# Moving the return of the last five token tiles into the first expert's work, the exponential to ScalarE, and the gather into the routing

## The chip, the cores and the metric

The kernel runs on one core of a Trainium2 chip. The metric is the time of one execution in device microseconds (us). A core has five engines, each with an instruction queue of its own that runs strictly in order: TensorE (PE in the profile; PEld is its weight load), VectorE (DVE), ScalarE (ACT), GpSimd (POOL), and SyncE (SP), which here only issues transfers. Transfers run on 16 DMA engines that all queues share.

## The reference

Three stages follow one another on inputs of B=4 sequences, H=8 heads, S=576 positions, D=64:

```python
# 1. attention: a local band of +-3 positions, plus attention over groups of 4 averaged positions
out_d     = softmax(scale * q_d @ k_d.T) @ v_d          # q_d, k_d, v_d: means of 4 positions
out_local = softmax(where(|i-j| < 4, scale * q @ k.T, -1e9)) @ v
x = (repeat(out_d, 4) + out_local) -> rows of N = 2304 tokens by 512
# 2. mixture of 8 experts, two for each token, with noisy gates
logits = x @ w_gate + log1p(exp(x @ w_noise)) * noise
x = sum over the two largest of softmax(two) * (relu(x @ w1[e]) @ w2[e])      # w1 512x1024, w2 1024x512
# 3. mixture of 8 other experts, one for each token
logits = x @ w_gate2 + modality_bias[modality_id]
out = gate * (relu(x @ w1'[e]) @ w2'[e])
```

## The kernel before

**Attention.** The loop at L1114 takes 18 steps; step i prepares head pair i+1, scores pair i and finishes pairs i-1 and i-2. Four pairs make a sequence, two pairs a group g for the loads. The order within a step is written by hand: `transposes(i+1)`, `softmax2(i-1)`, `values(i-2)`, `scores(i)`, `combine(i-2)`, `p_transposes(i-1)`, `softmax1(i)`, `softmax_d1/d2(i)`, and `pool_v`, GpSimd's sum of v over four positions. The result of a sequence collects in `xT` (features by tokens) and is whole after `combine` of its fourth pair.

**Giving x back.** The 18 tiles of 128 tokens go from `xT` to rows. `xback_att(t)` multiplies a tile by `gw` (an identity beside the two gate matrices) with 8 fp32 matmuls, or 16 where a tile spans two sequences, into `px`, which comes from the same pool of two buffers, `psD`, as the scores' `pd`. Its `rest()` runs at the next `flush()`: ScalarE copies the rows to `xr` (two buffers), VectorE sums the logits into `lg`, and a transfer writes `xr` to `x_rows` in DRAM. Before, the dictionaries `before` and `behind` say at which step a tile comes ahead of the scores or at the step's end; tiles 13 to 17 need the last sequence and come after the loop, at L1184.

**Routing.** `route1(c0, c1, ...)` is a generator that emits the routing of half of the tokens in small pieces. `tick(n)` takes n pieces; `Between` wraps VectorE, so that most attention instructions on it are followed by one piece. A piece that yields "PE" holds the generator until `unblock` lets TensorE's part in. Its parts: `softplus` on VectorE, with an exponential by a polynomial; the two largest; `places` on TensorE; `locate`; then 18 pairs of one-hot tiles (`hots`; for the first half `ol` is made on GpSimd, L545) which TensorE inverts into a table. `places_early` decodes the row numbers `idx0` of the first four experts' first 256 tokens, chosen from tiles 0 to 8 alone.

**Experts.** `ffn.run` goes through items, each one expert with some rows, 8 blocks f of F. Its first item has 256 rows, gathered by `ffn.gather` (GpSimd's indirect transfers) from `x_rows`. A block loads and splits weights into `whi`, `wlo`, does `layer1` of the next block and `layer2` of this one; `hook(i, f, half)` is called after `layer1` (half 0), in the middle of `layer2` (half 2) and after it (half 1). In the first four items `hook0` ticks the routing of the second half of the tokens, which must be done before the fifth item gathers its rows.

Of the kernel before, what the change touches and what calls it, by code (L numbers as in the profile page):

```python
# [18 lines left out]
MAGIC = 12582912.0  # L19
M128 = 1610612736.0  # L20

EXP = [1.0, 1.0000000360960746, 0.4999999535047545, 0.1666642092713234, 0.04166772440021678, 0.00837476549703475,
       0.0013859289912904367]
ATANH = [2.0, 0.666664104680626, 0.40021790854867745, 0.2799817325801463, 0.2802763957015976]


# [20 lines left out]
class Attention:  # L47
# [128 lines left out]
        if g % 2 == 0:  # L176
            self.xT[g // 2] = self.xpool.tile([128, 4, self.S], F32, tag="xT", name="xT")

    def pool_v(self, g, part):

        vr, vd = self.gt[g]["vr"], self.gt[g]["vd"]
        for c in range(2):
            self.nc.gpsimd.tensor_tensor(vd[:, c], vd[:, c] if part else vr[c][:, :, 0], vr[c][:, :, part + 1], op=ALU.add)

    def transposes(self, i):
# [157 lines left out]
def softplus(nc, V, pool, z, out, T, E):  # L343

    A = ALU

    def t(n, dt=F32):
        return pool.tile([128, 9, E], dt, tag=f"sp_{n}", name=f"sp_{n}")[:, :T]
    na, n, m, r, p, u, ni = t("na"), t("n"), t("m"), t("r"), t("p"), t("u"), t("ni", I32)

    V.scalar_tensor_tensor(na, z, -1.0, z, op0=A.mult, op1=A.min)
    yield
    V.tensor_scalar(na, na, -86.0, None, op0=A.max)
    yield
    V.tensor_scalar(n, na, 1.4426950408889634, MAGIC, op0=A.mult, op1=A.add)
    yield
    V.tensor_scalar(n, n, MAGIC, None, op0=A.subtract)
    yield
    V.scalar_tensor_tensor(r, n, -0.693359375, na, op0=A.mult, op1=A.add)
    V.tensor_scalar(m, n, 127.0, 8388608.0, op0=A.add, op1=A.mult)  # L360
    yield
    V.scalar_tensor_tensor(r, n, 2.12194440e-4, r, op0=A.mult, op1=A.add)
    V.tensor_copy(ni, m)
    yield
    V.tensor_scalar(p, r, EXP[6], None, op0=A.mult)
    yield
    for k in range(5, 0, -1):
        V.scalar_tensor_tensor(p, p, EXP[k], r, op0=A.add, op1=A.mult)
        yield
    V.scalar_tensor_tensor(p, p, 1.0, ni.bitcast(F32), op0=A.add, op1=A.mult)  # L370
    yield

    V.tensor_scalar(u, p, 2.0, None, op0=A.add)
    yield
    nc.vector.reciprocal(u, u)
    yield
    V.tensor_tensor(r, p, u, op=A.mult)
    yield
    V.tensor_tensor(u, r, r, op=A.mult)
    yield  # L380
    V.tensor_scalar(p, u, ATANH[-1], None, op0=A.mult)
    yield
    for c in ATANH[-2:0:-1]:
        V.scalar_tensor_tensor(p, p, c, u, op0=A.add, op1=A.mult)
        yield
    V.scalar_tensor_tensor(p, p, 2.0, r, op0=A.add, op1=A.mult)
    yield
    V.scalar_tensor_tensor(out, z, 0.0, p, op0=A.max, op1=A.add)
    yield
# [482 lines left out]
def core(ctx, tc, q, k, v, moe_w_gate, moe_w_noise, moe_noise, moe_w1, moe_w2,  # L872
# [42 lines left out]
    with ExitStack() as actx:  # L915
# [65 lines left out]
        def xback_att(t):  # L981
            px = att.psD.tile([128, 2, 512], F32, tag="D", name="px")
            pv = px[:, :, :2 * XB].rearrange("p a (b c) -> p a b c", b=2)
            xr = xback(t, [pv[:, 0], pv[:, 1]])

            def rest():
                nc.scalar.activation(xr, pv[:, :, :, :128], AF.Copy)
                nc.vector.tensor_reduce(lg[:, t], pv[:, :, :, 128:].rearrange("p a b c -> p c a b"), axis=AX.XY, op=ALU.add)
                nc.sync.dma_start(x_rows[128 * t:128 * t + 128, :DM], xr.rearrange("p a b c -> p (a b c)"))
            after.append(rest)  # L990

        def route1(c0, c1, bank, eng, heng, then=None):
# [101 lines left out]
        def places_early():  # L1094

            v, f = (t.rearrange("p (e t) -> p e t", e=E)[:, :NX, :NE0] for t in (tab, fs))
            yield from rt.decode(f, v, rt.padh.rearrange("p (e t) -> p e t", e=E)[:, :NX, :NE0])
            nc.vector.tensor_copy(idx0[:, 0], f)

            d = route.tile([128, NX, NE0], F32, tag="hold2", name="hold2")  # L1100
            nc.vector.tensor_scalar(d, f, float(N), -float(N), op0=ALU.is_ge, op1=ALU.mult)
            yield
            nc.vector.tensor_tensor(idx0[:, 1], d, f, op=ALU.add)
            yield

        att.tick = tick
        NP = 4 * B

        before = {6: 0, 7: 2, 10: 5, 11: 7, 14: 10, 15: 12}
        behind = {6: 1, 7: 3, 9: 4, 10: 6, 11: 8, 13: 9, 14: 11}  # L1110
        small = load_small()
        finish_now(att.transposes(0))
        att.group(0)
        for i in range(NP + 2):  # L1114
            g, ph = divmod(i, 2)
            if ph == 1:
                if g + 2 < 2 * B:
                    att.load_qk(g + 2)
                if g + 1 < 2 * B:
                    att.load_vr(g + 1)  # L1120
            if ph == 0 and i and g < 2 * B:
                att.load_vw(g)
            if 3 <= i <= 7:
# [12 lines left out]
                att.values(i - 2)  # L1136
                att.scale_d(i - 2)
            flush()
            if i == 12:
                back.append(route1(0, HT, att_bank, nc.vector, nc.gpsimd, hold))  # L1140
                back.append(places_early())
            unblock(1)
            if i in before:
                xback_att(before[i])
            if 0 < i < NP:
                att.scores(i)
            if i >= 2:
                att.combine(i - 2)
            flush()
            tick(2)  # L1150
            if 1 <= i <= NP:
                pt = att.p_transposes(i - 1)
                next(pt)
            if 0 < i < NP:
                att.softmax1(i)
            if 1 <= i <= NP:
                finish_now(pt)
            unblock(1)
            if i < NP:
# [1 line left out]
                if ph == 0 and g + 1 < 2 * B:  # L1161
                    att.group(g + 1)
                att.softmax_d2(i)
                for j in ((0, 1), (2,))[ph] if i > 1 else ((), (0, 1, 2))[ph]:
                    att.pool_v(g, j)
            tick(2 if i < NP else 30)
            if i == 9:
                second_bias()
            if i in behind:
                xback_att(behind[i])  # L1170
            if i == 12:

                nc.sync.dma_start(x_rows[N:].rearrange("(a p) c -> p a c", p=128),
                                  zero[:, None, :].to_broadcast([128, 5, XW]))
            if i == 14:
# [1 line left out]
                           [(e, EARLY) for e in range(NX)] + [(e, 640 - EARLY) for e in range(NX)]  # L1177
                           + [(e, 640) for e in range(NX, E)]]
                          + [dict(ns=n, w1=moe2_w1, w2=moe2_w2) for n in [512, 256, 256, 384] + [256] * (STATIC - 1)])

                nc.sync.dma_start(x2_rows.rearrange("(a p) c -> p a c", p=128),
                                  zero[:, None, :YW].to_broadcast([128, NT + 5, YW]))
        ffn.start()
        for t in range(13, NT):  # L1184
            xback_att(t)
            tick(3)
            flush()
            unblock(1)
            tick(6)
        tick(1000, True)  # L1190
        rows0 = ffn.gather(x_rows[:HT * 128, :], [idx0[:, 1, 0, j:j + 1] for j in range(NE0)], "xg0", NE0, axr)
    fpool = ctx.enter_context(tc.tile_pool(name="fpool", bufs=1))
    fps = ctx.enter_context(tc.tile_pool(name="fps", bufs=1, space=PSUM))
    ffn.open(fpool, fps)
# [74 lines left out]
    def ffn_bank():  # L1269
        return fps.tile([128, 512], F32, tag="y3", name="rbank")  # L1270

    def hook0(i, f, half):
        if i == 0 and half == 0 and f == 0:
            back.append(route1(HT, NT, ffn_bank, nc.vector, None))
            back.append(places_known())
        unblock(1)
        tick(1)

# [392 lines left out]
```

## Time and profile before

| | |
|---|---|
| median of three executions | 925.9 us (923.14 to 927.91) |
| the profiled execution | 926.93 us, span 925.2 us |
| busy | PE 94%, PEld 83%, DVE 59%, ACT 46%, POOL 35% |
| mean granted TensorE clock | 0.973 |
| first matmul of the first expert | at 179.99 us of the span |

The page's busy shares are means over stages. The attention and the first routing fill the span up to about 169 us; then come the last five tiles and the first gather, and from 180 us on the experts, with TensorE busy nearly throughout. What the change touches lies between 57 and 270 us.

### The profile page before, as it was taken

To read this page: it belongs to the slowest core of one execution; us is meant where nothing else is said; L and a number is where in the kernel's file an instruction comes from. 1 tells how busy PE (TensorE), PEld (TensorE's weight loads), DVE (VectorE), ACT (ScalarE), POOL (GpSimd) and SP (SyncE) were. 2 spreads that over 40 slices of the span, in tenths; PEclk is the share of its full clock that TensorE was granted. 3 is DMA by queue.
4 is the path that set the end of the run, shared out by engine and by line. 5 is a ranking of instruction groups with operands and counts; after the bars stand their busy time and mean duration, and the time that the engine had idled before them with its cause. 6 is when DMAs were issued, how large, how long until landed. Compare 5 with 4: busy or idle time off the path is not lost. (4 is left out here: it accounts for less than half of the span.)

```text
span 925.2 us, 18236 instructions
## 1 busy us (share of the span) xinstructions
PE 870.4 (94%) x6775; PEld 764.1 (83%) x6775; DVE 550.4 (59%) x1345; ACT 429.0 (46%) x947; POOL 322.3 (35%) x460
## 2 busy tenths in 40 slices
PE   5898977799999999999999999989989999999995
PEld 4777866698888988999898999978867889999994
DVE  6775697489975544554343443434666877556662
ACT  3675644455554534444233342334423356455552
POOL 7876658436553213043106032050020442222210
PEclk9998988899999999999999999999989999999998
DMA  8878659747776457476328245175433467546650
GB/s 175 171 159 189 169 143 329 240 167 229 204 235 195 140 146 181 143 204 147 129 71 182 92 92 162 46 161 161 128 99 109 155 239 245 190 154 220 216 209 24
DMA packets 158702, 153.83 MB, mean 166 GB/s; under 512 B 74319, under 2 KB 119887, under 8 KB 158608
## 3 DMA queue, kind: packets, MB, share of 16 engines
q1 hardware_dynamic: 146528, 120.15, 42.2%
q0 software_dynamic: 12080, 32.45, 15.2%
q8 instruction: 56, 0.92, 0.4%
q14 instruction: 38, 0.31, 0.1%
HBM read 124.98 MB, written 27.85 MB: 165 GB/s over the span
## 5 line engine op out<-in xcount | busy, mean ns | idle before, releaser
L746 PE MATMUL ph<-xh,whi 128*128 128x256 f32 (+3 forms) x768 | 238.4, 310 | 2.8 <-DVE wlo L707 2.1
L746 PE MATMUL ph<-xl,whi 128*128 128x256 f32 (+3 forms) x768 | 237.6, 309 | 0.4 <-DVE xl L732 0.3
L746 PE MATMUL ph<-xh,wlo 128*128 128x256 f32 (+3 forms) x768 | 237.6, 309 | 0.1
L758 PE MATMUL y<-whi,hh 128*128 128x512 f32 x472 | 192.2, 407 | 0.1
L758 PE MATMUL y<-wlo,hh 128*128 128x512 f32 x472 | 188.1, 398 | 0.0
L758 PE MATMUL y<-whi,hl 128*128 128x512 f32 x472 | 187.6, 398 | 0.0
L707 DVE TENSOR_TENSOR wlo<-raw,whi 128x512 fp32r<-128x512 f32 x135 | 93.2, 690 | 157.4 <-ACT whi L706 144.9
L706 ACT ACTIVATE whi<-raw 128x512 fp32r<-128x512 f32 x160 | 101.0, 631 | 170.7 <-PE y L758 155.7
L746 PEld LDWEIGHTS ph<-xh,whi 128*128 128x128 f32 x768 | 146.0, 190 | 12.2 <-issue 2.6
L746 PEld LDWEIGHTS ph<-xl,whi 128*128 128x128 f32 x768 | 145.9, 190 | 8.3 <-DVE xl L732 1.0
L748 ACT ACTIVATE hh<-ph 128x256 fp32r<-128x256 f32 (+3 forms) x192 | 83.2, 433 | 142.3 <-PE ph L746 133.0
L746 PEld LDWEIGHTS ph<-xh,wlo 128*128 128x128 f32 x768 | 146.2, 190 | 1.8 <-DVE wlo L707 0.3
L749 DVE SCALAR_TENSOR_TENSOR hl<-ph,hh 128x256 fp32r<-128x256 f32 (+3 forms) x192 | 92.5, 482 | 84.5 <-ACT hh L748 81.0
L1215 POOL DMA_INDIRECT x_rows<-y,idx x35 | 57.4, 1641 | 208.1 <-ACT y L1206 108.2
L709 DVE TENSOR_TENSOR wlo<-raw,whi 128x512 fp32r<-128x512 f32 x160 | 120.6, 754 | 11.9 <-ACT whi L708 10.9
L758 PEld LDWEIGHTS y<-whi,hl 128*128 128x128 f32 x472 | 89.5, 190 | 21.6 <-DVE hl L749 0.4
L758 PEld LDWEIGHTS y<-whi,hh 128*128 128x128 f32 x472 | 90.2, 191 | 13.6 <-DVE y L1208 0.8
L758 PEld LDWEIGHTS y<-wlo,hh 128*128 128x128 f32 x472 | 89.8, 190 | 12.6
L708 ACT ACTIVATE whi<-raw 128x512 fp32r<-128x512 f32 x160 | 98.6, 616 | 0.0
L732 DVE TENSOR_TENSOR xl<-pt,xh 128x512 fp32r<-128x512 f32 x59 | 38.7, 687 | 30.8 <-ACT xh L731 30.6
L271 POOL TENSOR_TENSOR Pd<-pe,sm 32x380 f32<-32x380 f32 (+1 forms) x48 | 42.1, 877 | 42.8 <-ACT kT L198 10.4
L1215 POOL DMA_INDIRECT out_dram<-y,pi x19 | 20.6, 1084 | 100.6 <-ACT y L1206 44.1
(311 smaller groups left out, 1085.5 us busy)
## 6 DMA issues: line engine op xcount, KB each, us to landing
raw<-in_moe_w_dram SPq DMA_DIRECT2D x160, 512.0 KB
x_rows<-zero SPq DMA_DIRECT2D x1, 5934.0 KB
vr<-in_v_dram SPq DMA_DIRECT2D x16, 288.0 KB
x_rows<-xr SPq DMA_DIRECT2D x18, 256.0 KB
x2l<-x_rows SPq DMA_DIRECT2D x18, 256.0 KB
qk<-in_q_dram SPq DMA_DIRECT2D x32, 128.0 KB
qk<-in_k_dram SPq DMA_DIRECT2D x32, 128.0 KB
vw<-in_v_dram SPq DMA_DIRECT2D x24, 128.0 KB
```

What stands on the lines that cost most here:

```text
L271: eng.tensor_tensor(Pd[s, :, W * g:W * g + n], pe[s, :, :n], sm[s, :, None].to_broadcast([W, 2 * NB, n]), op=ALU.mult)
L706: nc.scalar.activation(h1, a, AF.Copy)
L707: eng.tensor_tensor(l1, a, h1.bitcast(F32), op=ALU.subtract)
L708: nc.scalar.activation(hi[:, 1], r2[:, half], AF.Copy)
L709: nc.vector.tensor_tensor(lo[:, 1], r2[:, half], hi[:, 1].bitcast(F32), op=ALU.subtract)
L732: nc.vector.tensor_tensor(xl, p, xh.bitcast(F32), op=ALU.subtract)
L746: nc.tensor.matmul(ps, w[a][:, k], x[b][:, k, s], start=(i == 0), stop=(i == 3 * KD - 1))
L748: nc.scalar.activation(hh[:, s], ps, AF.Relu)
L749: nc.vector.scalar_tensor_tensor(hl[:, s], ps, 0.0, hh[:, s].bitcast(F32), op0=ALU.max, op1=ALU.subtract)
L758: nc.tensor.matmul(p, h[a][:, 128 * j:128 * j + 128], w[b], start=(f == 0 and i == 0), stop=(f == self.FB - 1 and i == 2))
L1215: d = nc.gpsimd.indirect_dma_start(out=dst, out_offset=bass.IndirectOffsetOnAxis(ap=ix, axis=0), in_=y, in_offset=None, **kw)
```

## The change

- `softplus`: the polynomial and its splitting are replaced by one ScalarE exponential, with three empty pieces after it.
- `rest()` issues the write of `xr` from ScalarE's queue and no longer from SyncE's.
- `between` takes the place of `before` and `behind`: a step's first tile comes between `scores(i)` and `p_transposes(i-1)`, a second one behind `softmax1(i)` and a flush.
- Tiles 13 to 17 leave the end of the attention: `hook0` gives them back in blocks 0 and 1 of the first item, in the banks y2 and y3; the second routing is queued after tile 17.
- `places_early` issues the gather of the first item itself; the first routing is queued at the end of step 12 and not in its middle.
- The zeros of `x2_rows` are written at step 12 and not at step 14; `load_vr` comes ahead of `load_qk`; `pool_v` does one half of the positions in each of the two steps of a group.

```diff
@@ class Attention
-    def pool_v(self, g, part):
+    def pool_v(self, g, c):
         vr, vd = self.gt[g]["vr"], self.gt[g]["vd"]
-        for c in range(2):
+        for part in range(3):
             self.nc.gpsimd.tensor_tensor(vd[:, c], vd[:, c] if part else vr[c][:, :, 0], vr[c][:, :, part + 1], op=ALU.add)
@@ def softplus
     V.scalar_tensor_tensor(na, z, -1.0, z, op0=A.mult, op1=A.min)
     yield
-    V.tensor_scalar(na, na, -86.0, None, op0=A.max)
-    yield
-    V.tensor_scalar(n, na, 1.4426950408889634, MAGIC, op0=A.mult, op1=A.add)
...
-    for k in range(5, 0, -1):
-        V.scalar_tensor_tensor(p, p, EXP[k], r, op0=A.add, op1=A.mult)
-        yield
-    V.scalar_tensor_tensor(p, p, 1.0, ni.bitcast(F32), op0=A.add, op1=A.mult)
-    yield
+    nc.scalar.activation(p, na, AF.Exp)
+    for _ in range(3):
+        yield
@@ def xback_att, rest()
-                nc.sync.dma_start(x_rows[128 * t:128 * t + 128, :DM], xr.rearrange("p a b c -> p (a b c)"))
+                nc.scalar.dma_start(x_rows[128 * t:128 * t + 128, :DM], xr.rearrange("p a b c -> p (a b c)"))
@@ def places_early
             nc.vector.tensor_tensor(idx0[:, 1], d, f, op=ALU.add)
+            rows0.extend(ffn.gather(x_rows[:HT * 128, :], [idx0[:, 1, 0, j:j + 1] for j in range(NE0)], "xg0", NE0, axr))
             yield
@@ the loop of the attention
-        before = {6: 0, 7: 2, 10: 5, 11: 7, 14: 10, 15: 12}
-        behind = {6: 1, 7: 3, 9: 4, 10: 6, 11: 8, 13: 9, 14: 11}
+        between = {6: [0], 7: [1], 8: [2], 9: [3], 10: [4, 5], 11: [6, 7], 12: [8], 14: [9], 15: [10], 16: [11], 17: [12]}
...
             if ph == 1:
+                if g + 1 < 2 * B:
+                    att.load_vr(g + 1)
                 if g + 2 < 2 * B:
                     att.load_qk(g + 2)
-                if g + 1 < 2 * B:
-                    att.load_vr(g + 1)
...
-            if i == 12:
-                back.append(route1(0, HT, att_bank, nc.vector, nc.gpsimd, hold))
-                back.append(places_early())
             unblock(1)
-            if i in before:
-                xback_att(before[i])
             if 0 < i < NP:
                 att.scores(i)
             if i >= 2:
                 att.combine(i - 2)
             flush()
             tick(2)
+            for t in between.get(i, [])[:1]:
+                xback_att(t)
             if 1 <= i <= NP:
                 pt = att.p_transposes(i - 1)
                 next(pt)
             if 0 < i < NP:
                 att.softmax1(i)
+            flush()
+            for t in between.get(i, [])[1:]:
+                xback_att(t)
             if 1 <= i <= NP:
                 finish_now(pt)
...
-                for j in ((0, 1), (2,))[ph] if i > 1 else ((), (0, 1, 2))[ph]:
-                    att.pool_v(g, j)
+                for c in ((0,), (1,))[ph] if i > 1 else ((), (0, 1))[ph]:
+                    att.pool_v(g, c)
             tick(2 if i < NP else 30)
...
-            if i in behind:
-                xback_att(behind[i])
             if i == 12:
+                flush()
+                back.append(route1(0, HT, att_bank, nc.vector, nc.gpsimd, hold))
+                back.append(places_early())
+                nc.sync.dma_start(x2_rows.rearrange("(a p) c -> p a c", p=128),
+                                  zero[:, None, :YW].to_broadcast([128, NT + 5, YW]))
                 nc.sync.dma_start(x_rows[N:].rearrange("(a p) c -> p a c", p=128),
                                   zero[:, None, :].to_broadcast([128, 5, XW]))
             if i == 14:
...
-                nc.sync.dma_start(x2_rows.rearrange("(a p) c -> p a c", p=128),
-                                  zero[:, None, :YW].to_broadcast([128, NT + 5, YW]))
+        flush()
         ffn.start()
-        for t in range(13, NT):
-            xback_att(t)
-            tick(3)
-            flush()
-            unblock(1)
-            tick(6)
         tick(1000, True)
-        rows0 = ffn.gather(x_rows[:HT * 128, :], [idx0[:, 1, 0, j:j + 1] for j in range(NE0)], "xg0", NE0, axr)
@@ hook0
+    T0 = 13
+    def xback_ffn(t):
+        px = [fps.tile([128, 512], F32, tag=f"y{2 + a}", name="px") for a in range(2)]
+        pv = [p[:, :2 * XB].rearrange("p (b c) -> p b c", b=2) for p in px]
+        xr = xback(t, pv)
+        for a in range(2):
+            nc.scalar.activation(xr[:, a], pv[a][:, :, :128], AF.Copy)
+        l2t = route.tile([128, 2, 2 * E], F32, tag="l2t", name="l2t")
+        for a in range(2):
+            nc.vector.tensor_reduce(l2t[:, a], pv[a][:, :, 128:].rearrange("p b c -> p c b"), axis=AX.X, op=ALU.add)
+        nc.vector.tensor_tensor(lg[:, t], l2t[:, 0], l2t[:, 1], op=ALU.add)
+        nc.scalar.dma_start(x_rows[128 * t:128 * t + 128, :DM], xr.rearrange("p a b c -> p (a b c)"))
+        if t == NT - 1:
             back.append(route1(HT, NT, ffn_bank, nc.vector, None))
             back.append(places_known())
     def hook0(i, f, half):
-        if i == 0 and half == 0 and f == 0:
+        t = T0 + 3 * f + (0, 2, 1)[half]
+        if i == 0 and t < NT:
+            xback_ffn(t)
         unblock(1)
         tick(1)
```

## Rows read from the trace of the kernel before

**Rows 1.** Windows: length; PE, PEld, DVE, ACT, POOL busy; granted clock; DMA share; GB/s.
```profile
75.20:87.50 12.30, 8.94 (x150) 7.22 (x148) 7.02 (x21) 6.27 (x22) 7.59 (x10) 0.81 0.89 217
113.80:147.90 34.10, 26.45 (x469) 22.26 (x468) 31.18 (x100) 17.61 (x58) 19.73 (x26) 0.90 0.62 176
147.90:168.70 20.80, 16.64 (x222) 13.42 (x220) 15.31 (x53) 8.98 (x26) 18.07 (x25) 0.84 0.99 340
180.00:206.90 26.90, 26.75 (x162) 24.42 (x163) 19.02 (x44) 13.66 (x27) 8.42 (x8) 0.90 0.60 208
```

**Rows 2.** Timeline of PE: start, duration, line, count, idle before and its releaser.
```profile
53.39 1.31 PE L285 MATMUL pp<-gw,Pd 128*128 128x128 f32 x10 [1.54 <-POOL Pd L271]
...
91.72 1.74 PE L971 MATMUL px<-gw,xT 128*64 128x144 f32 x16
...
105.69 1.25 PE L971 MATMUL px<-gw,xT 128*128 128x144 f32 x8
...
140.53 0.34 PE L213 MATMUL pd<-mask,identB 128*128 128x190 bf16 x2 [1.13 <-DVE lg L988]
...
177.83 1.48 PE L729 MATMUL pt<-gw,xg 128*128 128x128 f32 x8 [3.09 <-DVE lg L988]
179.99 0.58 PE L746 MATMUL ph<-xh,whi 128*128 128x256 f32 x1 [0.69 <-ACT xh L731]
```

**Rows 3.** Timeline of ACT, in the same form.
```profile
55.33 0.53 ACT L235 ACTIVATE pe<-pe 128x380 f32<-128x380 f32 x1
...
66.73 0.65 ACT L987 ACTIVATE xr<-px 128x512 f32<-128x512 f32 x1
...
79.80 0.60 ACT L987 ACTIVATE xr<-px 128x512 f32<-128x512 f32 x1 [4.25 <-DMA x_rows<-xr]
...
146.72 0.26 ACT L1014 ACTIVATE qex<-qex 128x72 f32<-128x72 f32 x1
...
172.59 0.60 ACT L987 ACTIVATE xr<-px 128x512 f32<-128x512 f32 x1 [1.96 <-PE px L971]
...
176.92 0.60 ACT L987 ACTIVATE xr<-px 128x512 f32<-128x512 f32 x1 [1.88 <-DMA x_rows<-xr]
```

**Rows 4.** Timeline of SP's queue: when it issued transfers.
```profile
74.02 0.83 SPq L989 DMA_DIRECT2D x_rows<-xr  x2
...
142.63 0.48 SPq L1181 DMA_DIRECT2D x_rows<-zero  x1
```

**Rows 5.** Timeline of DVE.
```profile
117.00 0.69 DVE L353 TENSOR_SCALAR sp_na<-sp_na 128x72 f32<-128x72 f32 x1
...
124.21 0.22 DVE L370 SCALAR_TENSOR_TENSOR sp_p<-sp_p,sp_ni 128x72 f32<-128x72 f32 x1
...
143.53 0.22 DVE L1011 TENSOR_TENSOR qex<-qnl,tpm 128x72 f32<-128x72 f32 x1
...
146.95 0.27 DVE L515 TENSOR_REDUCE more<-A 128x8 f32<-128x72 bf16 x1
...
168.48 0.17 DVE L1103 TENSOR_TENSOR idx<-hold,fs 128x8 int32<-128x8 f32 x1
```

**Rows 6.** Timeline of POOL.
```profile
146.00 1.78 POOL L545 TENSOR_SCALAR ol<-r_h,lclo 128x128 f16<-128x128 f16 x3 [2.39 <-DVE lclo L536]
147.86 2.81 POOL L271 TENSOR_TENSOR Pd<-pe,sm 32x380 f32<-32x380 f32 x3
...
161.94 4.91 POOL L545 TENSOR_SCALAR ol<-r_h,lclo 128x128 f16<-128x128 f16 x8
169.57 1.39 POOL L720 DMA_INDIRECT xg<-x_rows,idx  x1 [2.72 <-DVE wlo L707]
...
176.54 0.20 POOL L805 COPY meta<-xg 128x16 f32<-128x16 f32 x1 [2.29 <-DMA xg<-x_rows,idx]
```

**Rows 7.** Groups of instructions by line, up to 420 us: busy, mean ns.
```profile
L183 POOL TENSOR_TENSOR vd<-vd,vr 72x256 f32<-72x256 f32 x32 | 22.5, 724 | 0.0
```

**Rows 8.** DMA issues: KB each.
```profile
x_rows<-zero SPq DMA_DIRECT2D x1, 5934.0 KB
```

More of the change, by code (lines that the diff above doesn't have):

```diff
@@ L20 @@
 M128 = 1610612736.0
-EXP = [1.0, 1.0000000360960746, 0.4999999535047545, 0.1666642092713234, 0.04166772440021678, 0.00837476549703475,
-       0.0013859289912904367]
 ATANH = [2.0, 0.666664104680626, 0.40021790854867745, 0.2799817325801463, 0.2802763957015976]
@@ L348, in t @@
         return pool.tile([128, 9, E], dt, tag=f"sp_{n}", name=f"sp_{n}")[:, :T]
-    na, n, m, r, p, u, ni = t("na"), t("n"), t("m"), t("r"), t("p"), t("u"), t("ni", I32)
+    na, r, p, u = t("na"), t("r"), t("p"), t("u")
     V.scalar_tensor_tensor(na, z, -1.0, z, op0=A.mult, op1=A.min)
     yield
-    V.tensor_scalar(na, na, -86.0, None, op0=A.max)
-    yield
-    V.tensor_scalar(n, na, 1.4426950408889634, MAGIC, op0=A.mult, op1=A.add)
-    yield
-    V.tensor_scalar(n, n, MAGIC, None, op0=A.subtract)
-    yield
[L359 to L366, printed above, removed]
-    for k in range(5, 0, -1):
-        V.scalar_tensor_tensor(p, p, EXP[k], r, op0=A.add, op1=A.mult)
+    nc.scalar.activation(p, na, AF.Exp)
+    for _ in range(3):
         yield
-    V.scalar_tensor_tensor(p, p, 1.0, ni.bitcast(F32), op0=A.add, op1=A.mult)
-    yield
     V.tensor_scalar(u, p, 2.0, None, op0=A.add)
@@ L1103, in places_early @@
             nc.vector.tensor_tensor(idx0[:, 1], d, f, op=ALU.add)
+            rows0.extend(ffn.gather(x_rows[:HT * 128, :], [idx0[:, 1, 0, j:j + 1] for j in range(NE0)], "xg0", NE0, axr))
             yield
+        rows0 = []
         att.tick = tick
         NP = 4 * B
-        before = {6: 0, 7: 2, 10: 5, 11: 7, 14: 10, 15: 12}
-        behind = {6: 1, 7: 3, 9: 4, 10: 6, 11: 8, 13: 9, 14: 11}
+        between = {6: [0], 7: [1], 8: [2], 9: [3], 10: [4, 5], 11: [6, 7], 12: [8], 14: [9], 15: [10], 16: [11], 17: [12]}
         small = load_small()
@@ L1270, in ffn_bank, with hook0 @@
         return fps.tile([128, 512], F32, tag="y3", name="rbank")
-    def hook0(i, f, half):
-        if i == 0 and half == 0 and f == 0:
+    T0 = 13
[11 more added lines that the diff above has]
+        if t == NT - 1:
             back.append(route1(HT, NT, ffn_bank, nc.vector, None))
             back.append(places_known())
+    def hook0(i, f, half):
+        t = T0 + 3 * f + (0, 2, 1)[half]
+        if i == 0 and t < NT:
+            xback_ffn(t)
         unblock(1)
```

## The prediction

> **What bounds the kernel now.** I read the page first, then windows by stage, then the timelines of the stretch the change touches, engine by engine, and the SP queue. TensorE is the bound from about 180 us on: in the first expert it is busy 26.75 of 26.9 us [rows 1], so anything added there costs its own time. Before that no single engine is. The attention's steps are a ring of in-order queues: TensorE transposes, VectorE reduces and normalises, GpSimd scales the band (L271), TensorE transposes that, and so on; TensorE waits for GpSimd once a step, 1.54 us in the step shown [rows 2]. From 113.8 to 147.9 us VectorE is the bound, 31.18 of 34.1 us, because the first routing runs on it beside the attention; from there to 168.7 us it is GpSimd, 18.07 of 20.8 us [rows 1]. The row numbers for the first expert are ready at 168.48 + 0.17 = 168.65 us [rows 5], the second of its two gathered tiles is there at 176.54 us [rows 6], and its first matmul starts at 179.99 us [rows 2]. So the path to 179.99 is attention ring, VectorE, GpSimd, gather; the last five tiles lie beside the gather, and only their last 1.3 us (176.54 to 177.83, a wait for `lg`) are on it.
>
> **The change, part by part.** I follow that path and sum the shifts of the first expert's start, then add what the moved tiles cost behind it.
>
> *Steps 6 to 11: -1.8 us (bounds -7 and +4).* Four things.
> (a) ScalarE stood 4.25 us, until 79.80 us, for a buffer of `xr` [rows 3]. The copy that filled the buffer's predecessor had ended at 66.73 + 0.65 = 67.38 us, but SP, busy with the loads of q, k and v, issued its write only at 74.02 us [rows 4]. Issued by ScalarE it leaves 6.6 us earlier, and the wait goes: -4.25. In that stretch the granted clock was 0.81 of full speed, between the 1.2 and 2.4 GHz levels [rows 1]; without the stop I give 0.9 us back as an estimate (12.3 us at 0.19 less speed is 2.3 us of TensorE's time, of which TensorE is not all the step): -0.9.
> (b) Five tiles of these steps stood at a step's end, ahead of the next transposes, at up to 1.25 us [rows 2]. Between scores and band transposes a tile lies in the wait of up to 1.54 us for GpSimd [rows 2]. I take 0.6 us a tile, under half of either: -3.0 (0 to -6.2).
> (c) Now ScalarE copies `xr` and issues the write ahead of its later work in a step, where in even steps the next reductions wait for it. A copy is 0.6 [rows 3], an issue 0.83/2 = 0.4 on SP [rows 4]; no row shows an issue on ScalarE, so 0.3 to 0.9 on the path, twice in single-tile even steps; I take 0.9: +1.8.
> (d) In steps 10 and 11 the second tile finds only one free buffer of `psD`, that of the first tile, since `pd` of this step is still to be read by `softmax_d1`. It waits until ScalarE has passed the exponential, which ends 55.33 + 0.53 - 53.39 = 2.5 us after the band transposes start [rows 2, 3], then 0.6 of `xr` and some 0.3 of `lg`, 3.4 us in all; 1.15 of them TensorE fills with those transposes. +2.2 a step: +4.4 (0 if buffers come otherwise).
> Sum: -4.25 - 0.9 - 3.0 + 1.8 + 4.4 = -1.95; I take -1.8.
>
> *Steps 12 to 14: -7.1 us (bounds -10 and -3).* From the polynomial go 14 VectorE instructions, the first at 117.00, the last at 124.21 us [rows 5], 5.07 us in sum; they overlap by about 0.07 each, so 4.1 us of a saturated engine. In their place ScalarE does one exponential of the same shape as L1014's, 0.26 us [rows 3], hidden in ScalarE's idle half (17.61 of 34.1 us busy) and, for VectorE, behind the three empty pieces; if ScalarE came late, VectorE would stand up to 0.5 us. The routing now starts at the end of step 12, so that its 11 instructions of placing (143.53 to 146.95 us, 2.65 us in sum, 1.9 without overlap) [rows 5] come behind the normalisation of pair 14 and no longer ahead of it. The wait of the scores for `lg`, 1.13 us [rows 2], goes with the tile ahead of them. -4.1 - 1.9 - 1.1 = -7.1.
>
> *GpSimd's tail: +2.1 us (bounds 0 and +4).* From the band scaling at 147.86 us on, GpSimd is full [rows 1]. Three one-hot tiles that ran before it, 1.78 us [rows 6], now come behind it, and so does one more `pool_v` addition, 0.72 us [rows 7], since each step now does three of one half; of the sum, 2.5, I let 0.4 fall into its remaining idle time. Queued behind these on GpSimd are the other one-hot tiles (the last eight take 4.91 us [rows 6]) and then the gather itself, so this is on the path.
>
> *Row numbers to first matmul: -2.3 us (bounds -3.3 and -0.5).* Before: 179.99 - 168.65 = 11.34. The issue by the routing gains nothing by itself: before, GpSimd started the gather 0.92 us after the numbers were ready, with nothing of its own in between. Gone are the 1.3 us until `lg` frees the banks, and the five writes that shared the DMA engines with the second gather. I take 7.0 for the gather (7.89 before) and 2.0 for transposes and splits (2.16 before): 9.0.
>
> So the first expert starts 1.8 + 7.1 - 2.1 + 2.3 = 9.1 us earlier.
>
> *Tiles 13 to 17 in the first expert: +7.1 us (bounds +6 and +17).* TensorE is full there. Tile 13 spans two sequences, 16 matmuls, 1.74 us; four tiles of 8 matmuls are 1.25 each [rows 2]: 6.7. Each needs the banks of the one before; half a `layer2` lies between, so I add 0.4 of stalls. VectorE (19.02 of 26.9 us busy) and ScalarE (13.66) have room [rows 1]. The clock is low for the first part of the expert either way (mean 0.90 [rows 1]), since TensorE stands for the gather in both: 0, perhaps 1.5 either way.
>
> *At nothing:* the second softplus, because TensorE covers VectorE there (26.75 of 26.9 us; were VectorE the bound, up to 4.1 us would be won); the second routing queued four hooks later but with nine pieces less; loads of v ahead of q and k, since SP runs steps ahead; weights of blocks 4 and 5 issued earlier, as TensorE did not wait for weights.
>
> *Sum:* -9.1 + 7.1 = -2.0. The profiled execution, 926.9, becomes 924.9; the median of the runs shown lies 1.0 below that execution, so I predict **924.0 us**.
>
> On (a) the Trainium skill has a rule that speaks against the change: "DMA: Bandwidth & Descriptors", section "Issuing engines are not separate DMA queues", says that all issuers share the same DMA engines and that a second issuer saves only the sequencer's time, usually small. Here the row agrees on the flight but not on "small": of 12.4 us from the copy's end to 79.80, 6.6 were the line at SP. By the rule taken at its word the wait would stay; that is rival four.
>
> **The rivals.**
> 1. *The ring closes up.* (d) does not happen or is filled, and the routing, no longer against a full VectorE, saves more: -5 and -9, within their bounds, in the first two terms instead of -1.8 and -7.1, total -7. For it: TensorE was busy 26.45 of 34.1 us there, so there is room. Against: GpSimd's tail is full already. Time 919.
> 2. *ScalarE held by its own writes in the first expert (slower).* A tile's copy needs the `xr` buffer of two tiles before. A write took 176.92 - 173.19 = 3.7 us from its copy's end to its release [rows 3]. If tiles follow at some 2 us (an estimate: 1.25 and half a `layer2`), the third to fifth each wait; behind the copy stand ScalarE's `whi` and `hh`, and TensorE soon after them. Three full waits are 11.1 us in place of 0.4: total +8.7, 934.6. It decides from a flight above some 5 us, since expert work between the tiles hides about that.
> 3. *The zeros come down on v.* 5.9 MB [rows 8] at 340 GB/s [rows 1] hold the DMA engines for 17.5 us. Before they were issued at 142.63 us [rows 4], beside nothing urgent; now ahead of the last group's loads of v. If these land late, `pool_v` holds GpSimd in step 14, perhaps 5 us: total +3, 929.
> 4. *Writes no sooner.* The 4.25 + 0.9 us of (a) stay: total +3.1, 929.
>
> **How the numbers follow.** 0.5% is 4.6 us, about what a measurement of this kernel can tell from no change. My forecast, own range 919.5 to 928, has 0.40; 0.11 of that lies under 921.3: faster 0.11, same 0.29. Rival 1 has 0.29, nearly all faster: 0.28 and 0.01. Rival 2 has 0.14, slower 0.13, same 0.01. Rival 3 has 0.08, same 0.05, slower 0.03. Rival 4 has 0.09, same 0.06, slower 0.03. Faster 0.39, same 0.42, slower 0.19. The range takes in rival 1 with the bounds of its terms, down to 914.5, and rivals 3 and 4, and stops short of rival 2's full price: to 931.
>
> **What would show it.** The writes of `xr` on ScalarE's queue within 1 us of the copy, and no 4 us wait; scores spaced evenly from step 12 to 15; the row numbers near 162 us; the first L746 matmul near 171 us; in the first expert three tiles in block 0, two in block 1, and the expert's end about 2 us earlier than before. The prediction is wrong if TensorE stands for ScalarE between the tiles, if GpSimd waits for `vr`, or if the routing's end does not move with the attention.

## The result

The changed kernel takes **933.25 us** (median of 6, 929.28 to 936.64), the kernel before beside it 926.89 us: ratio 1.0071, 95% interval 1.0049 to 1.0094. It is slower, by some 6.6 us; the forecast was 924.0 with a range up to 931.0. The execution profiled after took 936.64 us (span 934.9), its own slowest; that of before 926.93 (span 925.2). So stages below add up to +9.7 us, and comparisons of time go by ratios.

The windows of the changed kernel, cut at the scores of steps 6, 12 and 15, at the row numbers, and at the first expert (columns as in [rows 1]):

```profile
60.75:119.88 59.13, 50.96 (x949) 43.41 (x948) 36.66 (x102) 35.54 (x118) 37.78 (x48) 0.97 0.77 191
119.88:151.67 31.79, 24.25 (x455) 20.49 (x454) 24.63 (x73) 15.92 (x54) 18.38 (x23) 0.91 0.87 292
151.67:176.31 24.64, 18.19 (x224) 16.17 (x223) 15.60 (x64) 9.41 (x28) 18.41 (x27) 0.77 0.34 111
185.44:218.60 33.16, 32.84 (x210) 29.83 (x211) 21.09 (x50) 17.24 (x38) 9.43 (x10) 0.92 0.44 151
```

I read every run by the same five landmarks: the starts of the scores' second group of matmuls (`pd<-kT,qT`) in steps 6, 12 and 15, the end of the last `idx<-hold,fs` (row numbers), the first `layer1` matmul, the first `y<-y` on ScalarE (first expert's end). Lengths between them, each in one profiled execution, in us (the stretch from the scores of step 15 to the row numbers is called the tail below):

| kernel | 6 to 12 | 12 to 15 | 15 to row numbers | to first matmul | first expert | ratio to before (95%) |
|---|---|---|---|---|---|---|
| before | 54.63 | 37.21 | 17.35 | 11.34 | 27.07 | 1 |
| changed | 59.13 | 31.79 | 24.64 | 9.13 | 33.19 | 1.0071 (1.0049-1.0094) |
| e1 old places | 51.05 | 32.40 | 25.46 | 8.87 | 33.13 | 1.0026 (1.0012-1.0040) |
| e2 late copy | 63.25 | 31.10 | 25.69 | 9.11 | 32.46 | 1.0139 (1.0117-1.0161) |
| e3 exponential alone | 50.97 | 32.33 | 17.22 | 11.80 | 26.27 | 0.9922 (0.9904-0.9941) |
| e4 five tiles alone | 51.03 | 38.47 | 17.22 | 8.55 | 32.67 | 1.0040 (1.0025-1.0054) |
| e5 old places, zeros | 50.77 | 33.24 | 23.15 | 8.88 | 33.03 | 0.9994 (0.9973-1.0016) |
| e6 old places, queueing | 50.97 | 29.96 | 26.41 | 9.11 | 33.43 | 1.0002 (0.9987-1.0018) |
| e7 old places, zeros, queueing | 50.72 | 32.09 | 18.50 | 8.72 | 33.65 | 0.9926 (0.9895-0.9957) |
| e8 five tiles back | 61.96 | 32.01 | 22.07 | 14.12 | 27.20 | 1.0085 (1.0056-1.0113) |
| e9 second tiles behind | 55.93 | 32.78 | 25.35 | 9.42 | 33.15 | 1.0025 (1.0005-1.0045) |
| e10 exponential, writes | 54.16 | 33.31 | 17.23 | 14.63 | 26.78 | 0.9977 (0.9958-0.9996) |
| e11 exponential, hots split | 54.29 | 31.92 | 16.22 | 12.12 | 27.58 | 0.9881 (0.9859-0.9902) |
| e12 as e7, five tiles back | 51.27 | 31.77 | 18.63 | 14.82 | 26.38 | 0.9920 (0.9898-0.9941) |
| e13 zeros only | 57.53 | 32.41 | 21.88 | 8.82 | 32.46 | 1.0087 (1.0066-1.0109) |
| e14 exponential, late queueing | 53.78 | 32.82 | 21.97 | 11.47 | 26.25 | 0.9941 (0.9920-0.9963) |

Names in the lines below: `Pd` is the band's softmax as GpSimd scales it, `pdT` ScalarE's copy of the transposed dilated softmax, `mxd` the maxima of the dilated scores, `vr` v as loaded and `vd` its sum over four positions, `vw` v as loaded for the band, and `ol` the one-hot tiles, made from `lclo`, a part of each token's place.

Three readings of the changed kernel. First TensorE's timeline; the rows with tiles and waits answer to [rows 2].

```profile
67.11 0.66 PE L193 MATMUL pk<-gw,qk 128*128 128x128 f32 x4 [0.94 <-ACT pdT L294]
...
76.47 0.76 PE L309 MATMUL pva<-pdT,vd 72*64 72x144 f32 x6 [0.88 <-ACT pdT L294]
...
102.96 1.25 PE L952 MATMUL px<-gw,xT 128*128 128x144 f32 x8 [1.90 <-DVE lg L969]
...
113.81 1.25 PE L952 MATMUL px<-gw,xT 128*128 128x144 f32 x8 [1.90 <-DVE lg L969]
...
180.45 1.09 PE L710 MATMUL pt<-gw,xg 128*128 128x128 f32 x4 [5.91 <-DMA xg<-x_rows,idx]
183.65 1.11 PE L710 MATMUL pt<-gw,xg 128*128 128x128 f32 x4 [2.11 <-DMA xg<-x_rows,idx]
185.44 0.58 PE L727 MATMUL ph<-xh,whi 128*128 128x256 f32 x1 [0.69 <-ACT xh L712]
...
190.99 1.74 PE L952 MATMUL px<-gw,xT 128*64 128x144 f32 x16
```

Then ScalarE's in step 6 (answers to [rows 3]):

```profile
65.62 0.61 ACT L968 ACTIVATE xr<-px 128x512 f32<-128x512 f32 x1
66.25 0.35 ACTq L970 DMA_DIRECT2D x_rows<-xr  x1
66.65 0.70 ACT L294 ACTIVATE pdT<-ppd 72x288 f32<-72x288 f32 x2 [0.42 <-ACT xr L968]
```

The tile's copy and the issue of its write stand 1.03 us ahead of `pdT`, for which TensorE waits: 0.94, 0.88, 0.92, 0.87 us in steps 6 to 9, once each. The 4 us wait for an `xr` buffer is gone, as forecast.

Last GpSimd's (answers to [rows 6]):

```profile
149.35 3.21 POOL L269 TENSOR_TENSOR Pd<-pe,sm 32x380 f32<-32x380 f32 x3 [2.87 <-DVE sm L40]
...
154.19 1.79 POOL L526 TENSOR_SCALAR ol<-r_h,lclo 128x128 f16<-128x128 f16 x3 [0.43 <-DVE lclo L517]
...
158.26 3.66 POOL L526 TENSOR_SCALAR ol<-r_h,lclo 128x128 f16<-128x128 f16 x6
162.00 2.54 POOL L269 TENSOR_TENSOR Pd<-pe,sm 32x380 f32<-32x380 f32 x3
...
167.70 4.69 POOL L526 TENSOR_SCALAR ol<-r_h,lclo 128x128 f16<-128x128 f16 x8 [1.35 <-PE rbank L532]
176.61 1.40 POOL L701 DMA_INDIRECT xg<-x_rows,idx  x1 [4.22 <-DVE idx L1084]
```

All ten one-hot tiles of the first batch now come behind the `Pd` of 149.35; before, three of the ten ran ahead of the `Pd` of 147.86 [rows 6]. Nine of them stand ahead of the last `Pd`. The gather leaves at 176.61, in [rows 6] at 169.57.

### The profile page after: what moved, and what is told of

It reads as the page before. It is cut to its first block, busy times and chain, and to the rows that moved or that the text cites. A ratio compares the mean times of both kernels' runs of the same rounds, so it can differ in the third digit from the quotient of the medians.

```text
span 934.9 us, 18191 instructions
## 1 busy us (share of the span) xinstructions
PE 871.1 (93%) x6775; PEld 764.1 (82%) x6775; DVE 544.4 (58%) x1327; ACT 430.5 (46%) x954; POOL 322.8 (35%) x460
## 3 DMA queue, kind: packets, MB, share of 16 engines
q0 software_dynamic: 12080, 32.45, 14.8%
## 5 line engine op out<-in xcount | busy, mean ns | idle before, releaser
L690 DVE TENSOR_TENSOR wlo<-raw,whi 128x512 fp32r<-128x512 f32 x160 | 119.9, 749 | 12.5 <-ACT whi L689 10.7
```

The source lines that it names most:

```text
L690: nc.vector.tensor_tensor(lo[:, 1], r2[:, half], hi[:, 1].bitcast(F32), op=ALU.subtract)
```

## The experiments

"Ratio" is always to the kernel before, beside it on the same chip.

**e1: tiles 0 to 12 at their old places.**

```diff
-        between = {6: [0], 7: [1], 8: [2], 9: [3], 10: [4, 5], 11: [6, 7], 12: [8], 14: [9], 15: [10], 16: [11], 17: [12]}
+        before = {6: 0, 7: 2, 10: 5, 11: 7, 14: 10, 15: 12}
+        behind = {6: 1, 7: 3, 9: 4, 10: 6, 11: 8, 13: 9, 14: 11}
```

> Changed kernel, but tiles 0 to 12 stand where they stood before (ahead of the scores, or at a step's end); everything else of the change is kept. Theory A (where the tiles stand is what went wrong: the xr copy and its issue on ScalarE ahead of pdT cost about 0.9 us in each step with a tile, the second tile of steps 10 and 11 waits 1.9 us): scores(6) to scores(12), 54.6 us before and 59.1 in the changed kernel, becomes 50 to 53 us, since the 4.25 us wait for a buffer of xr stays gone; the time falls by 5 to 8 us to 925 to 928. Theory B (issuing a write on ScalarE costs its time wherever it stands): the stretch stays at 57 us or more, the time at 931 or more. Theory C (the zeros from step 12 and GpSimd's tail made it all): the stretch falls but the row numbers of the first expert do not come earlier than 174 us, time 931 to 934.

929.27 us, 1.0026. Steps 6 to 12 take 51.05 us, as theory A had it, with the writes still on ScalarE, so B falls: the places are worth 0.45% (1.0071 - 1.0026), some 4 us. But the stretch gave 8.1 and the time only half of that, for a new wait came up in GpSimd's timeline, shown with SP's queue:

```profile
144.24 0.73 POOL L181 TENSOR_TENSOR vd<-vr 72x256 f32<-72x256 f32 x1 [7.41 <-DMA vr<-in_v_dram]
```
```profile
117.97 0.40 SPq L1156 DMA_DIRECT2D x_rows<-zero  x1
118.41 10.31 SPq L1158 DMA_DIRECT2D x_rows<-zero  x1
128.82 5.47 SPq L142 DMA_DIRECT2D vr<-in_v_dram  x2
```

L1156 is the 5.9 MB of zeros that the change moved, L1158 a second write of zeros, of 1.3 MB, that was at step 12 before, too; its issue takes 10.31 us behind the first. The last group's v is issued behind both and GpSimd stands 7.41 us for it, with the band scaling and the one-hots queued behind.

**e2: the first tile's copy behind `pdT`.**

```diff
-            flush()
             for t in between.get(i, [])[1:]:
+                flush()
                 xback_att(t)
             if 1 <= i <= NP:
                 finish_now(pt)
+            flush()
```

> Changed kernel, but the first tile's copy of xr, its lg and its write are queued behind the pdT copies of the step instead of ahead of them (in the double steps the second tile still lets the first go first). Theory A: each single-tile step of 6 to 9 goes from 8.9 to about 8.0 us, scores(6) to scores(12) from 59.1 to about 55.5, the time falls by 2 to 4 us to 929 to 931. Theory B (issue on ScalarE costs wherever it stands): steps stay at 8.9 us, time 932 to 934.

938.85 us, 1.0139: slower than the changed kernel, outside both theories. `pdT` is no longer waited for, and two of the four single-tile steps take 8.5 us instead of 9.05; the other two take 8.98 and 10.09 (8.85 and 8.88 in the changed kernel). But `lg` waits for the copy on VectorE's queue, ahead of `mxd`, on which the dilated exponentials and then ScalarE's `kT` and `qT` depend. VectorE's timeline in steps 9 and 10:

```profile
92.43 0.22 DVE L969 TENSOR_REDUCE lg<-px 128x16 f32<-128x64 f32 x1 [3.42 <-ACT xr L968]
92.57 0.74 DVE L40 TENSOR_REDUCE mxd<-pd 72x4 f32<-72x576 f32 x1
...
105.20 0.23 DVE L969 TENSOR_REDUCE lg<-px 128x16 f32<-128x64 f32 x1 [3.76 <-ACT xr L968]
```

The interval from the scores of step 10 to those of step 11 became 15.3 us (11.4 in the changed kernel and in e13, but 14.3 in e8, and all three have the same program up to there, so that the interval alone decides nothing). The time does: the intervals of the two ratios lie apart. The order on ScalarE alone was too narrow a theory; that the loss now comes by VectorE's queue is argued from these waits and was not tested by itself.

**e3: the exponential alone**, in the kernel before.

```diff
-    V.tensor_scalar(na, na, -86.0, None, op0=A.max)
...
-    V.scalar_tensor_tensor(p, p, 1.0, ni.bitcast(F32), op0=A.add, op1=A.mult)
+    nc.scalar.activation(p, na, AF.Exp)
```

> Kernel before, with the exponential of the softplus on ScalarE and nothing else of the change. Theory A (VectorE is the bound from scores(12) to scores(15) and 14 instructions of 4.1 us leave it): row numbers at 164 to 166 us instead of 168.65, time lower by 2 to 4 us, 922 to 924. Rival (the ring of PE and GpSimd sets these steps, or GpSimd's tail does): row numbers within 1 us of 168.65, time within 1 us of 926.

919.21 us, 0.9922. More than theory A gave. Steps 12 to 15 go from 37.21 to 32.33 us, the tail keeps its 17.2. Up to step 12 the program is that of the kernel before, yet ScalarE's wait for a buffer of `xr`, 4.25 us in [rows 3], is 1.50 here:

```profile
78.58 0.60 ACT L970 ACTIVATE xr<-px 128x512 f32<-128x512 f32 x1 [1.50 <-DMA x_rows<-xr]
```

**e4: tiles 13 to 17 in the first expert and the gather by the routing**, in the kernel before.

```diff
-        for t in range(13, NT):
-            xback_att(t)
...
+        if i == 0 and t < NT:
+            xback_ffn(t)
```

> Kernel before, with tiles 13 to 17 in the first expert and the gather issued by the routing, and nothing else of the change (polynomial, places, writes of tiles 0 to 12, zeros as before). Theory A (the five tiles cost 6 to 7 us of a full TensorE and only some 2 us come back at the first matmul): first matmul 177 to 179 us instead of 179.99, first expert 33 us instead of 27, time 929 to 932. Rival (the later part of the first item gives the tiles back, because weights or routing wait there anyway): time 925 to 928.

929.74 us, 1.0040: theory A. The first expert takes 5.6 us more, the first matmul follows the row numbers 2.8 us sooner.

**e5, e6, e7: old places, and the zeros or the queueing of the routing put back, or both.**

```diff
 e5, e7
             if i == 12:
-                nc.sync.dma_start(x2_rows.rearrange("(a p) c -> p a c", p=128),
-                                  zero[:, None, :YW].to_broadcast([128, NT + 5, YW]))
...
             if i == 14:
...
+                nc.sync.dma_start(x2_rows.rearrange("(a p) c -> p a c", p=128),
+                                  zero[:, None, :YW].to_broadcast([128, NT + 5, YW]))
 e6, e7 (and no longer at the end of step 12)
             flush()
+            if i == 12:
+                back.append(route1(0, HT, att_bank, nc.vector, nc.gpsimd, hold))
+                back.append(places_early())
             unblock(1)
```

> Changed kernel with the places of tiles 0 to 12 of before and with the zeros of x2_rows issued in step 14 as before (in the run with the old places alone GpSimd stood 7.4 us for vr, the last group's v). Theory Z (the earlier zeros hold the last v): no wait of GpSimd for vr, from scores(15) to the row numbers 25.5 us becomes 18 to 20, time 922 to 925. Theory R (the routing queued half a step later sets the tail whatever the zeros do): the wait goes, but lclo stays near 34 us after scores(12) and the tail at 24 to 26 us, time 927 to 930.

> Changed kernel with the old places of tiles 0 to 12 and with the routing queued in the middle of step 12 as before; the zeros stay at step 12. Theory Z (zeros hold v): GpSimd still stands 6 to 8 us for vr, and the tail stays at 23 us or more, time 927 to 930. Theory R (the later queueing of the routing makes the tail): lclo 7 us earlier, the tail 18 to 20 us, time 922 to 925.

> Changed kernel with old places, old zeros and old queueing of the routing: what is left of the change is the exponential, the tiles 13 to 17 in the first expert with the gather by the routing, the writes of xr issued by ScalarE, and the order of the v loads and pool_v. Theory A (parts add up: exponential -6.7, five tiles +3.8, the rest nothing): 922 to 924. Rival (writes on ScalarE or pool_v cost something anywhere): 926 or more.

e5: 926.28 us, 0.9994; e6: 927.92 us, 1.0002; e7: 921.55 us, 0.9926, near theory A. From the scores of step 12 to the row numbers (columns 3 and 4) e7 takes 50.6 us, e5 56.4, e6 56.4, e1 57.9. Either of the two alone costs nearly as much as both. In e6 GpSimd stands for `vr`, as theory Z had it; in e5 it does not, but its first one-hot tile waits for `lclo`, as theory R had it, made at 146.78 us, 35.5 after the scores of step 12 (26.4 in e7). GpSimd's timelines in e6, then e5:

```profile
142.47 0.72 POOL L181 TENSOR_TENSOR vd<-vr 72x256 f32<-72x256 f32 x1 [7.66 <-DMA vr<-in_v_dram]
```
```profile
147.13 1.80 POOL L526 TENSOR_SCALAR ol<-r_h,lclo 128x128 f16<-128x128 f16 x3 [1.76 <-DVE lclo L517]
```

Both theories were right in mechanism and wrong in thinking that one was the cause: the two lie side by side, and taking away one leaves the other. In time, e1 to e7 is 1.0%, and the interval of e7 lies apart from those of e5 and e6.

**e8: in the changed kernel, tiles 13 to 17 back beside the gather.**

```diff
+        for t in range(13, NT):
+            xback_att(t)
...
-        if i == 0 and t < NT:
-            xback_ffn(t)
```

> Changed kernel with tiles 13 to 17 back beside the gather and the gather issued after the routing, everything else of the change kept. Theory A (the tiles cost 6 us in the expert and win 2 to 3 at the first matmul): first expert 27 us instead of 33, row numbers to first matmul 11 to 12 us instead of 9.1, time 929 to 931. Rival (with the late routing the tiles beside the gather run at the low clock and delay it by as much): 932 to 934.

934.84 us, 1.0085: the rival, just above its range; nothing was won. The expert is 6.0 us shorter, but the first matmul comes 14.1 us behind the row numbers and no longer 9.1.

**e9: in the changed kernel, tiles 5 and 7 at the step's end.**

```diff
-            for t in between.get(i, [])[1:]:
-                xback_att(t)
...
                 second_bias()
+            for t in between.get(i, [])[1:]:
+                xback_att(t)
```

> Changed kernel with only the second tile of steps 10 and 11 (tiles 5 and 7) moved from between to the step's end; all else of the change kept. Theory D (the double steps are what the places cost: scores(10) to scores(12) 23.3 us against 15.7 with the old places): that stretch becomes 16 to 18 us, the time falls by 3 to 6 us to 927 to 930. Rival (the copies ahead of pdT cost as much in the single steps, and VectorE's lg moves with them): the stretch stays above 20 us, time 931 or more.

931.11 us, 1.0025. Scores of step 10 to those of step 12: 20.1 us (23.3 in the changed kernel, 15.7 with the old places): by a hair the rival's figures, above 20 us and 931. The second tile accounts for somewhat under half of the loss in these steps; the rest is left with the first tile in its new place. In time e9 equals e1 (1.0025 and 1.0026), although e1 takes all the tiles back: e1 has the wait of 7.41 us for v, and e9 has none.

**e10: exponential and writes on ScalarE**, in the kernel before.

```diff
-                nc.sync.dma_start(x_rows[128 * t:128 * t + 128, :DM], xr.rearrange("p a b c -> p (a b c)"))
+                nc.scalar.dma_start(x_rows[128 * t:128 * t + 128, :DM], xr.rearrange("p a b c -> p (a b c)"))
```

> Kernel before with the exponential on ScalarE (as in the run of it alone, 919.2) and with the writes of tiles 0 to 12 issued by ScalarE. Theory N (the 4.25 us wait for xr was made up elsewhere in the ring, so that the issue brings nothing): within 1.5 us of the exponential alone, 917.5 to 921. Rival P (the wait was real, as the prediction had it): 914 to 916, steps 6 to 12 shorter by 3 us or more.

925.99 us, 0.9977: both theories missed, the writes cost 0.55%. Between the scores of steps 8 and 10 GpSimd stood for TensorE's values, then for v, and TensorE behind GpSimd:

```profile
83.64 0.73 POOL L183 TENSOR_TENSOR vd<-vr 72x256 f32<-72x256 f32 x1 [3.06 <-PE pva L317]
85.14 0.80 POOL L183 TENSOR_TENSOR vd<-vr 72x256 f32<-72x256 f32 x1 [0.77 <-DMA vr<-in_v_dram]
```
```profile
89.92 2.39 PE L285 MATMUL pp<-gw,Pd 128*128 128x128 f32 x10 [3.71 <-POOL Pd L271]
```

SP's loads come later: v is issued at 78.64 us, behind q and k, where e3 had issued it at 71.73. SP's queue now stands for the writes that ScalarE issues. Its waits from 55 to 100 us, as total, times and longest (L158 loads `vw`, L131 q and k):

```profile
SPq L158 <- DMA x_rows<-xr: 8.5, 2, 6.5
SPq L131 <- DMA x_rows<-xr: 3.4, 2, 2.8
```

The kernel before and e3 have no such wait. In the trace's records the transfers of both queues use the same eight landing semaphores (100 to 107) in turn: the write issued by ScalarE at 61.89 us and the load of `vw` that SP issues at 64.42 both have 106, and the load is held until the write has landed. How much of the 0.55% this makes is not shown. Another 2.8 us of the profile's difference lie beside the gather (first matmul 14.63 us behind the row numbers, 11.80 in e3).

**e11: exponential, and four of the last eight one-hot tiles on VectorE**, in the kernel before.

```diff
-                    ho.append(rt.hots(lo[:, j, c:c + 1], hi[:, j, c:c + 1], rt.code[:, c0 + c:c0 + c + 1], heng))
+                    ho.append(rt.hots(lo[:, j, c:c + 1], hi[:, j, c:c + 1], rt.code[:, c0 + c:c0 + c + 1],
+                                      None if len(todo) <= 10 and j else heng))
```

> Kernel before with the exponential on ScalarE and with four of the last eight one-hot tiles ol (0.59 us each on GpSimd) made by VectorE. Theory G (GpSimd bounds the tail to the row numbers): from scores(15) to the row numbers 15 to 16 us instead of 17.2, time 1 to 3 us under the exponential alone, 916 to 918. Rival (TensorE's one-hot matmuls and VectorE's table bound it, or the saved time is lost at the gather): within 1 us of 919.

917.13 us, 0.9881, theory G: the fastest, ahead of both kernels (against e3 1.0 us off the tail in the profile, 0.4% in time). Its ScalarE stands as long for `xr` as the kernel before did in [rows 3]:

```profile
79.28 0.60 ACT L970 ACTIVATE xr<-px 128x512 f32<-128x512 f32 x1 [4.44 <-DMA x_rows<-xr]
```

**e12: as e7, tiles 13 to 17 beside the gather**; the edit of e8 on e7.

> Changed kernel with old places, old zeros, old queueing of the routing, and tiles 13 to 17 beside the gather again: what is left is the exponential, the writes issued by ScalarE and the order of the v loads and pool_v. Theory A (parts add up, five tiles 3 to 4): first expert 27 us, time 2 to 4 us under the 921.6 with the tiles in the expert, 917.5 to 919.5. Rival (with an early routing the tiles cost as much beside the gather as in the expert): 920.5 to 922.

920.56 us, 0.9920: equal to e3 and, within the intervals, to e7; the rival. Here the tiles beside the gather hold the first expert up, by ScalarE's and TensorE's timelines:

```profile
173.53 0.60 ACT L968 ACTIVATE xr<-px 128x512 f32<-128x512 f32 x1 [5.18 <-DMA x_rows<-xr]
```
```profile
174.44 1.97 PE L710 MATMUL pt<-gw,xg 128*128 128x128 f32 x8 [6.13 <-DVE lg L969]
```

The two buffers of `xr` are in flight together with the gather; the fifth tile's copy waits 5.18 us and the transposes behind it 6.13. GpSimd stands 4.63 us for the second gathered tile, 1.88 in e3.

**e13: in the changed kernel, only the zeros back at step 14** (the first edit of e5).

> Changed kernel, tiles where the change put them, only the zeros of x2_rows back in step 14. In the changed kernel's trace GpSimd never stands for vr, while with the old places it stood 7.4 us. Theory W (the slow steps 10 and 11 make the v loads come in time, so that the zeros are not on the path here; the two losses cover each other): within 1.5 us of the changed kernel, 932 to 935. Rival Z (the zeros cost 3 us in any arrangement, by what they take from the DMA engines): 929 to 931.

935.08 us, 1.0087, 0.16% from the changed kernel and within the intervals: theory W. The zeros cost nothing that shows in the time where the attention is late anyway.

**e14: exponential, and the routing queued at the end of step 12**, in the kernel before (the second edit of e6 the other way).

> Kernel before with the exponential on ScalarE, and the routing queued at the end of step 12 instead of its middle; nothing else. Theory R (half a step of ticks is lost and the one-hots come behind the last band scaling on GpSimd): lclo 7 us later after scores(12), tail from scores(15) to the row numbers 22 to 25 us instead of 17.2, time 4 to 6 us over the exponential alone, 923 to 925.5. Rival S (steps 12 to 15 get shorter by what the placing no longer takes from VectorE there, as the prediction had it, 1.9 us and more): 918 to 921.

923.16 us, 0.9941, against 0.9922 for the exponential alone; by the ratios 1.8 us, by the profile 5.2 (12 to row numbers, 49.6 to 54.8). The two differ, and the intervals overlap. What the trace does show is where: GpSimd's first one-hots wait for `lclo` until 148.26 us, the last eight for TensorE:

```profile
148.26 1.80 POOL L528 TENSOR_SCALAR ol<-r_h,lclo 128x128 f16<-128x128 f16 x3 [1.76 <-DVE lclo L519]
...
161.26 4.70 POOL L528 TENSOR_SCALAR ol<-r_h,lclo 128x128 f16<-128x128 f16 x8 [1.82 <-PE rbank L534]
```

Steps 12 to 15 take 32.82 us, 32.33 without this edit: the placing that left VectorE there gave nothing (rival S falls in its mechanism, though the time by the ratio lies near its figure).

## Why the prediction was wrong

By the ratios the loss lies in three moves. Without the new places, the early zeros and the late queueing (e7) the change is at 0.9926, where the exponential alone is at 0.9922 (e3); with the zeros and the queueing it is at 1.0026 (e1), with the places too at 1.0071. So the zeros and the queueing cost 1.0% together, the places 0.45% on top of them, and the rest of the change brings nothing in sum beside the exponential.

**The step "Steps 6 to 11: -1.8 us" failed first.** They cost +4.5 in the profiled executions (54.63 to 59.13). One execution is a coarse measure here: with the same program up to step 12 the stretch took 50.97 to 54.63 us (before, e3, e4, e11, e14), and 57.53 to 61.96 with the changed one (changed, e8, e13).
- (a), -5.15 us, is the term that was misread. The wait vanished, but it had been worth little. In before, e3, e4, e11 and e14 ScalarE stood 4.25, 1.50, 1.74, 4.44 and 3.66 us there. The three long waits are those of executions whose step 6 came early: on average the wait is 2.5 us longer, the scores of step 6 are 2.4 us earlier, and those of step 12 only 0.8 later. In before and e3 the two writes leave SP at about the same time (74.02 and 73.79 us), and ScalarE is released at 79.80 and 78.58; the scores of step 8 were at 75.48 and 77.01. Whoever comes earlier waits longer. Hence 54.63 and 50.97 us between steps 6 and 12 are no difference of two kernels. With the old places and the writes on ScalarE (e1, e5, e6, e7, e12) the scores of step 12 come at 111.7 us on average, 113.1 in those five; 1.4 us of the 5.15 is all that shows, and single executions spread over 4. A wait read from one execution was booked as a gain.
- (b), -3.0 us, did not come. In the changed kernel two steps without a tile take 8.50 + 7.06 = 15.6 us, two with one tile each 17.9; with the old places (e1) steps 10 and 11 hold three tiles in 8.69 + 7.04 = 15.7. So three tiles at their old places cost some 0.1 us, and one at its new place 1.15, nearly the 1.25 that it lasts. Six steps without tiles would take 46.7 us, an estimate from the first sum; with eight tiles they take 51.05 at the old places and 59.13 at the new. The tile at a step's end, which I took for a cost, was covered there; the cover between scores and band transposes, which I took for free, did not serve.
- (c), +1.8, was mis-sized: I charged even steps alone, but TensorE stands 0.9 us for `pdT` in each of steps 6 to 9, 3.6 in all. What of it is cost is not shown: without these waits (e2) two of the four steps are 0.5 us shorter, and two longer.
- (d), +2.2 for each double step (2.1 with the 1.31 us that the transposes last in [rows 2], where I put 1.15): the wait is there, 1.90 us twice. With the first tile's delay and the tile itself the two steps take 23.3 us, with the old places 15.7.

**"GpSimd's tail: +2.1 us" failed next**: 17.35 to 24.64 us, +7.3. I charged what was moved on GpSimd and not when the routing would deliver. The half step that it is queued later keeps VectorE's `lclo` back, 26.7 us after the scores of step 12 in e3, 34.9 in e14, 34.0 in the changed kernel; the exponential's saving is lost in that. The zeros, rival 3, are the second limit beside it: 7.41 us of waiting in e1, none in the changed kernel, whose attention is later and finds v there. In the profiles the half step alone gives 4.8 of the 7.3 (e14 against e3), and 4.7 with the old places (e5 against e7), where it is 0.68% in time and the intervals lie apart. The rest was not taken apart; e13 and e8, at 21.9 and 22.1, have the tail of e14.

**"Steps 12 to 14: -7.1 us"** measured -5.4. The polynomial was right: -4.9 in e3, where 4.1 and a wait of 1.1 stood. The 1.9 for the moved placing were not there (e14).

**"Row numbers to first matmul: -2.3"** measured -2.2, and **"Tiles 13 to 17: +7.1"** +6.1. Both hold in e4 too. Their balance does not sum as simply: alone +0.40% (e4), +0.06% between e12 and e7, -0.14% between e8 and the changed kernel, the last two within the intervals. Where ScalarE issues the tiles' writes beside the gather, the first matmul comes 14.1 to 14.8 us behind the row numbers (e8, e10, e12), and 11.3 to 12.1 where SP does (before, e3, e11, e14); the place in the expert is then worth more.

So -1.8, -7.1, +2.1, -2.3, +7.1 became +4.5, -5.4, +7.3, -2.2, +6.1, sum +10.3; step 6 comes 1.3 us later, and behind the first expert 1.9 come back, for +9.7.

**The rivals.** Rival 1 fell: the ring did not close up, steps 6 to 12 got longer. Rival 2 named the right time, 934.6, by luck and the wrong mechanism: between tiles 13 to 17 TensorE stands 0.17 us at most for their release. Rival 4, that the writes bring nothing, is near what e12 against e3 shows (0.9920, 0.9922). It rested on the Trainium skill, "DMA: Bandwidth & Descriptors", section "Issuing engines are not separate DMA queues": a second issuer saves only sequencer time. Those two runs agree with it, and e10 (+0.55%) shows that it can cost. The reason for putting the order of the loads at nothing, that "SP runs steps ahead", did not allow for the writes on ScalarE: SP's queue stands for them to land, 23.4 us in all between 55 and 125 us in e10 and 11.6 in the changed kernel, none before. Left open: why e12 loses nothing by this (SP stands 12.5 us for the writes there, but v goes ahead of q and k, GpSimd does not stand for it, and `pool_v` differs too), and how the parts of e14's loss split.

## What to carry to other kernels

A stall in a ring of in-order queues is a gain only if the ring's next limit is farther off: compare the same stall in a second execution, or its whole stage, before booking it. Work given to a "free" slot needs a free slot on every queue that evacuates it, and a generator that starts half a step later delivers half a step later, whatever is cheaper in it. When two limits end together, undoing either one shows little; undo both. And ask what a moved transfer shares with those that stay: a queue can stand for a write that another engine issues.

## What the hardware showed unexpectedly

- An issue on ScalarE takes 0.33 to 0.40 us, and where nothing else is waited for 0.40 to 0.45 pass between the copy ahead of it and the next instruction, the issue included; with the copy's 0.61 that makes the 1.03 us (65.62 to 66.65 us in the changed kernel).
- Behind the 5.9 MB of zeros, whose own issue took 0.41 us, the next issue, 1.3 MB of zeros, held SP's queue for 8.06 us in the changed kernel and 10.31 in e1, although SP only issues; the loads behind it start that much later. Where the 5.9 MB come later (e13), the same 1.3 MB are issued in 0.41 us.
- Removing transfers from SP's queue moved its later loads back, not forward (e10: v at 78.64 us, 71.73 in e3): a load that takes the same landing semaphore as a write issued by ScalarE is held until that write has landed, 7.3 us in the longest case between 55 and 125 us.
